# A diffusion block on one core: prologue reordered with two modulation vectors inside it, mixer channels regrouped by shift group, a later w4 load, branch hints on all engines, the last tile in halves

## The chip, the cores and the metric

The kernel runs on one core of a Trainium2 chip. The metric is device time in microseconds (us) of a whole execution; the median of several runs is quoted. Each experiment was timed beside runs of the kernel before on the same chip.

The *span* is the time from the first to the last record of the profiled execution. The time of a run is some 4 to 6 us longer than its span; that difference is called the gap below.

## The reference, cut to what matters

```python
x = A_x                                              # [1, 2048, 640]
mod = (silu(c) @ w_mod).reshape(1, 6, 1, -1)         # six vectors of 640
sa, ca, ga, sb, cb, gb = ...                         # mod[:, 0] ... mod[:, 5]
h = layernorm(x) * (1 + ca) + sa
x = x + ga * attention(h, k_cache, v_cache, wq, wo)  # 32 heads of 128, 2048 keys
h = layernorm(x) * (1 + cb) + sb
u = gelu(layernorm(h) @ w1)                          # 640 channels in 4 groups of 160
u = shift each group by +1, -1, +2, -2 tokens        # group g0 g1 g2 g3
x1 = h + u @ w2
x = x + gb * (x1 + gelu(layernorm(x1) @ w3) @ w4)    # hidden width 1728
```

Two facts of it matter here. Vectors 0 and 1 of the modulation are wanted at once, vectors 2 to 5 only near the end. And a shift group has 160 channels, while a matmul result has 128 partitions, so groups and tiles don't line up.

## The kernel before: the parts that matter

The program is a list of operations with priorities. A small scheduler simulates the engines with assumed durations and fixes, ahead of time, **one order for each engine**; each operation then waits on the chip with semaphores. `slack` is a number of ns that the scheduler adds to the time at which it thinks an operation's inputs are ready; `need` and `from_slot(n)` hold a DMA back until the n-th exponential.

The attention is 128 *steps*: 8 groups of 4 heads, in each group 4 *chunks* of 512 queries, in each chunk 4 heads. A step has 8 pairs of score matmuls, 8 exponentials of 128x1024 on ScalarE, and the PV products.

```python
def ln1(ch, prio):                    # layer norm of chunk ch
    ...
        for i in (a, a + 1):
            ln_stats(xs[i].ap, ..., prio, 0.0 if ch == 0 else 2000.0)     # VectorE
        rstd_act(g, a, a + 2, prio - 100)                                 # ScalarE: Ln, then Exp
        for i in (a, a + 1):
            normed(xn[i].ap, ...)                                         # VectorE
    ...                               # chunk 0: transposes on TensorE; other chunks:
        for i in range(4):
            dmaT(... dma_start_transpose(hT_t[ch][:, :, i * 128:(i + 1) * 128], xn[i].ap), ...)   # SyncE queue
        for k in range(KT):           # VectorE: times (1 + ca), plus sa
            ... hT_t[ch][:, k, :] ...

MS = 17                               # modulation vectors 2, 4, 3, 5 from step 17 on
for n, p in enumerate((2, 4, 3, 5)):
    dma("SP", ... w_half[n % 2] <- w_mod[:, p * D:(p + 1) * D] ...)
    ...                               # 10 matmuls of 128x320 each

def mlp_in(ch, prio):                 # layer norms ahead of the mixer
    tail = ch == NC - 1
    def rstd(g, a):
        if tail:
            rstd_dve(g, a, a + 2, prio)            # last quarter: VectorE, no table
            shift(g, a, a + 2, prio)
        else:
            rstd_act(g, a, a + 2, prio, 1200.0)    # Ln and Exp on ScalarE
            negate(g, a, a + 2, prio, 1200.0)

TAIL = ("A0 WO B0 B1 B2 A1 B3 A2 B4 B5 B6 B7 C0 I3 D0 D1 D2 D3 C1 A3 ...").split()
# A = w1 of a quarter of the rows, B = w2 of a tile, C = w3, D = w4, WO = last attention output product

def w1_part(ch, key):
    for n in range(KT):               # 5 tiles of 128 channels
        ...                           # 5 matmuls of 128x512
        for (p0, p1, dl) in segs[n]:  # a tile is cut where a shift group ends: 9 pieces in all
            P.op("ACT", ... e.activation(us_ap[p0:p1, n, ch * QC + 2 + dl:...], m[p0:p1, :], GELU), ...)
```

Of the kernel before, what the change touches and what calls it, by code (L numbers as in the profile page):

```python
# [40 lines left out]
class Plan:  # L41
# [3 lines left out]
    ENG = ("PE", "ACT", "DVE", "POOL", "SP")  # L45

# [115 lines left out]
    def emit(self, nc, es, ndma, redo, flag):  # L162
# [68 lines left out]
        def body(e):  # L231
            def f(eng):
                for i, o in enumerate(self.seq[e]):
                    if e == "PE" and i == len(self.seq[e]) - 300:
                        hint[e] = eng.mark_branch_hint_location()
                    for sem, v in waits[o].items():
                        eng.wait_ge(sem, v)
                    ins = o.fn(eng)
                    if o.dma:
                        ins.then_inc(o.sem, 16)  # L240
                    elif o.needed:
                        ins.then_inc(o.sem, 1)
                eng.wait_ge(self.flag_op.sem, self.flag_op.semval)
                eng.load(redo[eng.engine], flag[0:1, 0:1])
                for sem in dsem.get(e, ()):
                    if fin.get(sem, 0) > know[e].get(sem, 0):
                        eng.wait_ge(sem, fin[sem])
            return f
# [10 lines left out]
def fast_path(nc, es, flag, A_x, A_k_cache, A_v_cache, A_wq, A_wo, B_w1, B_w2, B_w3, B_w4, c, w_mod, out):  # L259
# [9 lines left out]
    HG = 4  # L269
# [62 lines left out]
    us = [T() for _ in range(NC)]  # L332
# [16 lines left out]
    W12 = [T(), T()]  # L349
    w_half = [W12_t[:, i * KT * D:(i + 1) * KT * D].rearrange("p (k n) -> p k n", k=KT) for i in range(2)]  # L350
# [23 lines left out]
    def dma(eng, fn, kb, reads, writes, prio, need=()):  # L374
        return P.op(eng, fn, {"SP": 480, "ACT": 480, "POOL": 1000}[eng], reads, writes, prio, dma=True, kb=kb, need=need)
# [9 lines left out]
    for i in range(NKV):  # L385
        P.op("POOL", lambda e, i=i: e.memset(V_ap[i][:, :, 128:130], 1.0), 200, (), (V[i],), -297 + i)
# [16 lines left out]
    x0 = load_x2(0, -301) + load_x2(2, -301, eng="ACT")  # L403
# [29 lines left out]
    P.op("DVE", lambda e: e.tensor_copy(s_bc.ap, c_f.ap.unsqueeze(2).to_broadcast([128, KT, 128])), 800, (c_f,), (s_bc,), 0.5)  # L433
    spin(50, -298)
    for k in range(KT):
        def mcol(e, k=k):
            for j in range(2 * KT):
                ins = e.matmul(mc[:, j:j + 1], wm_ap[:, k, j * 128:(j + 1) * 128], s_bf[:, k:k + 1],
                               start=(k == 0 and j == 0), stop=(k == KT - 1), skip_group_check=True)
                if k < KT - 1:  # L440
                    dummy(e, 1)
            return ins
        P.op("PE", mcol, 2 * KT * 120, (wm[k], s_bf, ones), (mc,) + ((warm,) if k < KT - 1 else ()), -290 + k, accum=True)
    spin(12, -281)
# [83 lines left out]
    def ln1(ch, prio):  # L528
        g = ln_slot()
        xs = x0 if ch == 0 else load_x2(4 * ch, XP[ch], from_slot(XS[ch])) + load_x2(4 * ch + 2, XP[ch], from_slot(XS[ch]))  # L530
        for a in (0, 2):
            for i in (a, a + 1):
                ln_stats(xs[i].ap, (xs[i],), g, i, prio, 0.0 if ch == 0 else 2000.0)
            rstd_act(g, a, a + 2, prio - 100)
            for i in (a, a + 1):
                normed(xn[i].ap, xn[i], xs[i].ap, xs[i], g, i, False, prio - 1)
        raw = [T() for _ in range(4)]
        if ch == 0:
# [5 lines left out]
            for i in range(4):  # L544
                def tr(e, i=i):
                    for k in range(KT):
                        ins = e.transpose(hslice(k, i, i + 1), xn[i][:, k * 128:(k + 1) * 128], ident_t[:])
                    return ins
                P.op("PE", tr, 330, (xn[i], ident), (hp[0], hp[1], hq, hp[4]), -280 + i, accum=True)
                spin(6 if i < 3 else 10, -279.5 + i)  # L550
# [18 lines left out]
    def load_k(h, prio, gate=(), need=()):  # L569
        b = h % NKV  # L570
        for i in range(4):
            dmaT(lambda e, i=i: e.dma_start_transpose(K_ap[b][:, i * 512:(i + 1) * 512].unsqueeze(1), A_k_cache[0, h, i * 512:(i + 1) * 512, :]),
                 128, gate, (K[b][i],), prio + 0.01 * i, need)
# [5 lines left out]
    def load_wq(g, a, b, prio, need=()):  # L579
        dma("SP", lambda e: e.dma_start(wq_t[g % 2][:, :, a * 128:b * 128],  # L580
                                        A_wq[:, (g * HG + a) * 128:(g * HG + b) * 128].rearrange("(k p) d -> p k d", p=128)),
            160 * (b - a), (), tuple(wq[g % 2][a:b]), prio, need)
# [8 lines left out]
    load_k(0, -296)  # L591
    load_v(0, -290, "ACT", gate=(wm[3],))
    ln1(0, -280)

    def load_head(h):
# [3 lines left out]
        load_k(h, pr, need=from_slot(n))  # L599
        load_v(h, pr + 1, need=from_slot(n + 1))  # L600
# [6 lines left out]
    load_wq(0, 1, HG, -295)  # L607
# [4 lines left out]


    MS = 17
    for n, p in enumerate((2, 4, 3, 5)):
        dma("SP", lambda e, n=n, p=p: e.dma_start(w_half[n % 2], w_mod[:, p * D:(p + 1) * D].rearrange("(k p) n -> p k n", p=128)),
            800, (), (W12[n % 2],) + (tuple(wm) if n < 2 else ()), MS * NP - 30 + n, from_slot((MS + 2 * n) * NP - 20))
        for hf in range(2):
            m = Tile(pool="M")
            sl = slice(hf * HD, (hf + 1) * HD)  # L620
            for k in range(KT):
                i = (n * 2 + hf) * KT + k
                P.op("PE", lambda e, m=m, sl=sl, k=k, n=n: e.matmul(m[:, 0:HD], s_bc[:, k, :], w_half[n % 2][:, k, sl], start=(k == 0), stop=(k == KT - 1)),  # L623
                     MM(HD), (s_bc, W12[n % 2]), (m,), NP * (MS + i // KT) + 4 + i % KT + 0.65, accum=True)
            P.op("DVE", lambda e, m=m, p=p, hf=hf: e.tensor_scalar_add(out=mod[p][hf].ap, in0=m[:, 0:HD], scalar1=1.0 if p == 4 else 0.0),
                 490, (m,), (mod[p][hf],), NP * MS - 60)

    TAIL = ("A0 WO B0 B1 B2 A1 B3 A2 B4 B5 B6 B7 C0 I3 D0 D1 D2 D3 C1 A3 B8 B9 B10 B11 D4 D5 D6 D7 B12 B13 B14 B15 C2 "
            "D8 D9 D10 D11 C3 D12 D13 D14 D15").split()
    WOKEY = 3000 + 50 * TAIL.index("WO")  # L630
    WOD, CH, I3D = 0, -200, -200


    evac = []
# [13 lines left out]
    def wo_group(g, ch):  # L648
# [3 lines left out]
        for qt in range(4):  # L652
            dmaT(lambda e, qt=qt: e.dma_start_transpose(OT_ap[gs][:, qt], On_ap[gs][:, qt].rearrange("p h d -> p (h d)")),
                 128, (On[gs][qt // 2],), (OT[gs][qt],), s * NP - 100)
# [37 lines left out]
    def step(s):  # L692
# [5 lines left out]
        if s == 0:  # L698
            q_proj(0, [-270 + kk for kk in range(KT)])
            spin(8, -260)  # L700
# [96 lines left out]
    for i, w in enumerate((B_w1, B_w2)):  # L797
        dma("SP", lambda e, i=i, w=w: e.dma_start(w_half[i], w.rearrange("(k p) n -> p k n", p=128)), 800, (), (W12[i],), E)
# [3 lines left out]
    for i, (f0, f1, old) in enumerate(((0, 6, kv(0)), (6, 12, kv(0, 1)))):  # L802
        dma("SP", lambda e, f0=f0, f1=f1: e.dma_start(KV_t[:, f0 * D:f1 * D].rearrange("p (f n) -> p f n", n=D),
                                                      B_w4[f0 * 128:f1 * 128, :].rearrange("(f p) n -> p f n", p=128)),
            960, (), (w4[i],) + old, E + 11 + i)
# [6 lines left out]
    segs = []  # L812
    for n in range(KT):
        lst = []
        p = 0
        while p < 128:
            grp = (n * 128 + p) // G4
            pe_ = min(128, (grp + 1) * G4 - n * 128)
            while p < pe_:
                q1 = min(pe_, p + (128 if p == 0 else (64 if p == 64 else 32)))  # L820
                lst.append((p, q1, DEL[grp]))
                p = q1
        segs.append(lst)
    old = tuple(PT) + tuple(QT)
    P.op("POOL", lambda e: e.memset(us_ap[:, :, 0:4], 0.0), 300, (), (us[0],) + old, -1900)
    P.op("POOL", lambda e: e.memset(us_ap[:, :, UW - 4:UW], 0.0), 300, (), (us[NC - 1],) + old, -1900)

    def w1_part(ch, key):
        for n in range(KT):
            m = Tile(pool="T")  # L830
            for kk in range(KT):
                P.op("PE", lambda e, m=m, n=n, kk=kk: e.matmul(m.ap, w_half[0][:, kk, n * 128:(n + 1) * 128], nT_ap[ch][:, kk, :],  # L832
                                                               start=(kk == 0), stop=(kk == KT - 1)),
                     MM(QC), (W12[0],) + tuple(nT[ch]), (m,), key + n + 0.1 * kk, accum=True)
            for (p0, p1, dl) in segs[n]:
                P.op("ACT", lambda e, m=m, n=n, p0=p0, p1=p1, dl=dl: e.activation(  # L836
                    us_ap[p0:p1, n, ch * QC + 2 + dl:ch * QC + 2 + dl + QC], m[p0:p1, :], GELU), act(QC), (m,), (us[ch],), key)
# [5 lines left out]
    def w2_tile(t, key):  # L843
# [4 lines left out]
        for hf in range(2):  # L848
            for kk in range(KT):
                P.op("PE", lambda e, kk=kk, hf=hf: e.matmul(m[:, hf * 512:hf * 512 + HD], us_ap[:, kk, 2 + t * 128:2 + (t + 1) * 128],  # L850
                                                            w_half[1][:, kk, hf * HD:(hf + 1) * HD], start=(kk == 0), stop=(kk == KT - 1)),
                     MM(HD), tuple(us[x] for x in need) + (W12[1],), (m,), key + hf + 0.1 * kk, accum=True)
# [30 lines left out]
    def w4_tile(t, key):  # L883
        i = t % 4
        b = xb[t]
        m = Tile(pool="W")
        for hf in range(2):
            for f in range(NF):
# [3 lines left out]
                     MM(HD), (gT[f], w4_of(f), w4b), (m,), key + hf + 0.01 * f, accum=True)  # L892
        o_ = xin[t % 4]
# [16 lines left out]
    pr = 2500  # L910
    P.op("DVE", lambda e: e.tensor_reduce(out=fl[:, 0:1], in_=rl_t[:], op=ALU.max, axis=mybir.AxisListType.X), 650, (rl,), (fl,), pr)
    P.op("DVE", lambda e: e.tensor_reduce(out=fl[:, 1:2], in_=rl_t[:], op=ALU.min, axis=mybir.AxisListType.X), 650, (rl,), (fl,), pr)
# [4 lines left out]
    P.op("PE", lambda e: e.matmul(m[:, 0:1], ones.ap, flb.ap, start=True, stop=True), 60, (flb, ones), (m,), 3400)  # L917
# [710 lines left out]
def bass_adaLN_cond__mha_block_cached__mixer_s_mlp__prompt_kernel(  # L1628
    nc, A_x, A_k_cache, A_v_cache, A_wq, A_wo, B_x, B_w1, B_w2, B_w3, B_w4, c, w_mod, out,
):  # L1630
    with nc.sbuf_tensor("flag", [128, 1], I32) as flag:
# [5 lines left out]
        for e, eng in nc.engines.items():  # L1637
            br = eng.br_cmp(redo[e], 0, comp_op="IS_EQ", on_true="done", on_false="general")
            if eng is nc.tensor:
                br.branch_hint(hint["PE"])  # L1640
# [32 lines left out]
```

## Time and profile before

| | before |
|---|---|
| time, median of 3 runs | 1401.2 us |
| profiled run: time, span | 1400.64, 1395.0 us |
| TensorE busy | 1380.7 us |
| first Q projection starts | 14.20 us |
| Q projection of step 4 starts (no wait) | 45.38 us |
| first w1 matmul to last matmul ("the tail") | 1206.27 to 1390.51, 184.2 us |
| last matmul to end of span | 4.5 us |

The page of the profile, parts 1 and 4 (busy time and the chain that ended last), says that TensorE bounds the kernel:

```profile
PE 1380.7 (99%) x13176; PEld 939.8 (67%) x13176; DVE 518.0 (37%) x1337; ACT 1114.6 (80%) x1195; POOL 123.5 (9%) x106
...
PE 96%; ACT 2%; POOL 1%; DVE 0%; DMA 0%; issue 0%; ACTq 0%; POOLq 0%
```

So only what makes TensorE idle, or slow, counts. The view of waits on TensorE of the kernel before (line of code, what it waited for, us in total, times, longest) has little in it:

```profile
PE f_S L668 <- ACT f_PQ L836: 3.2, 1, 3.2
PE f_S L712 <- ACT f_PQ L714: 2.7, 3, 1.8
PE f_S L850 <- ACT f_PQ L836: 1.7, 1, 1.7
```

L836 is the GELU behind w1, in the tail. L712 is a score matmul that waited for an exponential, at 25.5 us.

Now the tail, first as a table of windows (window, its length, busy time and instructions of PE, PEld, DVE, ACT and POOL, granted clock, which is the share of full clock speed that TensorE got, DMA share, GB/s):

```profile
1210.00:1215.00 5.00, 1.83 (x9) 0.62 (x7) 1.08 (x3) 4.89 (x9) 2.51 (x3) 1.00 0.92 193
1215.00:1220.00 5.00, 4.58 (x23) 2.62 (x24) 2.78 (x6) 4.17 (x6) 2.25 (x2) 0.66 0.25 50
...
1230.00:1235.00 5.00, 3.28 (x20) 1.70 (x19) 3.99 (x13) 3.38 (x6) 0.00 (x0) 1.00 0.33 66
```

A window in which TensorE idles over 3 us is followed by one with a granted clock of 0.66; in finer windows that is 0.50 for 3.4 us, from 1215.6 to 1219.0, and 1.00 on both sides. The Trainium skill, "TensorE: Matmul & The Clock Gate", Part 1, says that after an idle window of about 3.4 us the clock is halved, and that the window is free-running; this agrees (3.2 us of waiting, then 3.4 us at 0.50). Half speed over 3.4 us costs at most 1.7 us (an estimate from these two numbers), so **this wait is paid for about one and a half times**. The timeline of the kernel before (start us, duration us, engine, line, operation, out<-in, count, idle time before and its releaser) shows what ScalarE did there:

```profile
1209.28 1.28 ACT L477 ACT_TABLE_LOAD   x1
...
1210.89 1.28 ACT L478 ACT_TABLE_LOAD   x1
...
1212.41 1.28 ACT L836 ACT_TABLE_LOAD   x1
...
1215.04 0.75 PE L668 MATMUL f_S<-f_wo,f_OO 128*128 128x320 bf16 x4 [3.22 <-ACT f_PQ L836]
```

L477 and L478 are Ln and Exp of the third quarter's layer norm. They stand between GELUs, and each of the three changes (to Ln, to Exp, back to GELU) loads a table for 1.28 us.

### The profile page before, as it was taken

The numbers are of one execution on the slowest core, as the hardware profiler recorded it, in microseconds if no ns is written. First come the engines' busy times: TensorE is split into PE (matmuls) and PEld (weight loads), VectorE is DVE, ScalarE is ACT, GpSimd is POOL, SyncE is SP. The second block draws the span as 40 slices with busy tenths as digits, with TensorE's granted clock in tenths as the row PEclk, the third lists the DMA queues.
The fourth block names the chain that finished last, engine by engine and source line by source line (L and its number), as shares of the span: only waits on it lengthen the run. The fifth ranks groups of instructions, "written<-read, shape, count | busy, mean of one in ns | idle before, by whom it ended". The sixth has DMA issues, their size and how long they took to land.

```text
span 1395.0 us, 29964 instructions
## 1 busy us (share of the span) xinstructions
PE 1380.7 (99%) x13176; PEld 939.8 (67%) x13176; DVE 518.0 (37%) x1337; ACT 1114.6 (80%) x1195; POOL 123.5 (9%) x106
## 2 busy tenths in 40 slices
PE   8999999999999999999999999999999999899998
PEld 6666676766676667666776677666766766555554
DVE  4453333233323332333223332333233345595552
ACT  5988888888888888888888888888888888864222
POOL 0000000000000000000000000001233376600000
PEclk9999999999999999999999999999999999999999
DMA  9551623261214221241215112612254112411110
GB/s 203 126 110 34 134 61 85 51 107 35 47 35 88 55 47 35 55 88 33 49 22 98 33 40 33 107 35 47 54 103 102 17 31 55 111 39 48 34 39 24
DMA packets 258963, 88.82 MB, mean 64 GB/s; under 512 B 236625, under 2 KB 257554, under 8 KB 258834
## 3 DMA queue, kind: packets, MB, share of 16 engines
q1 hardware_dynamic: 256210, 85.41, 30.1%
q8 instruction: 104, 1.70, 0.5%
q10 hardware_dynamic: 2624, 1.51, 0.5%
q14 instruction: 25, 0.20, 0.1%
HBM read 43.48 MB, written 2.62 MB: 33 GB/s over the span
## 4 chain that ended last, share of the span: by engine, by line
PE 96%; ACT 2%; POOL 1%; DVE 0%; DMA 0%; issue 0%; ACTq 0%; POOLq 0%
PE f_O L731 33%; PE f_S L712 31%; PE f_M L643 10%; PE f_M L668 10%; PE f_S L890 2%; PE f_M L890 2%; PE f_S L877 2%; PE f_O L877 2%; ACT f_PQ L836 1%; PE f_S L413 1%; PE f_S L850 1%; PE f_M L850 1%; POOL f_y L511 0%; PE f_S L832 0%; PE f_M L623 0%; DMA f_xin<-in_A_x_dram 0%
## 5 line engine op out<-in xcount | busy, mean ns | idle before, releaser
L714 ACT ACTIVATE f_PQ<-f_S 128x1024 bf16<-128x1024 f32 x1024 | 1030.2, 1023 | 155.0 <-PE f_S L712 147.6
L731 PEld LDWEIGHTS f_O<-f_KV,f_PQ 128*128 128x128 bf16 x8192 | 539.6, 98 | 211.4 <-ACT f_PQ L714 0.4
L731 PE MATMUL f_O<-f_KV,f_PQ 128*128 128x129 bf16 x8192 | 612.2, 220 | 0.2 <-ACT f_PQ L714 0.2
L712 PE MATMUL f_S<-f_PQ,f_KV 128*128 128x512 bf16 x2048 | 608.9, 379 | 3.1 <-ACT f_PQ L714 2.7
L676 DVE TENSOR_TENSOR f_y<-f_M,f_y 128x320 f32<-128x320 f32 x192 | 94.4, 492 | 524.8 <-PE f_M L668 524.8
L668 PE MATMUL f_M<-f_wo,f_OO 128*128 128x320 bf16 x992 | 270.2, 299 | 0.0
L712 PEld LDWEIGHTS f_S<-f_PQ,f_KV 128*128 128x128 bf16 x2048 | 192.0, 98 | 46.6 <-ACT f_PQ L714 3.9
L643 PE MATMUL f_M<-f_hT,f_wq 128*128 128x512 bf16 x640 | 159.2, 379 | 0.1
L511 POOL TENSOR_TENSOR f_y<-f_y,f_mod 128x640 f32<-128x640 f32 x40 | 61.3, 1542 | 1058.2 <-DVE f_y L676 1050.8
L668 PEld LDWEIGHTS f_M<-f_wo,f_OO 128*128 128x128 bf16 x992 | 94.9, 97 | 27.9
L643 PEld LDWEIGHTS f_M<-f_hT,f_wq 128*128 128x128 bf16 x640 | 62.4, 98 | 75.9 <-DVE f_hT L557 0.9
L740 DVE TENSOR_TENSOR f_OO<-f_O,f_rl 128x256 bf16<-128x256 f32 x256 | 108.4, 423 | 8.3
L646 DVE CAST f_PQ<-f_M 128x512 bf16<-128x512 f32 x128 | 88.5, 691 | 54.8 <-PE f_M L643 54.7
L738 DVE RECIPROCAL f_rl<-f_O 128x2 f32<-128x2 f32 x256 | 43.5, 170 | 45.9 <-PE f_O L731 41.7
L880 ACT ACTIVATE f_OO<-f_O 128x512 bf16<-128x512 f32 (+1 forms) x28 | 16.7, 596 | 33.2 <-PE f_O L877 33.1
L880 ACT ACTIVATE f_OO<-f_S 128x512 bf16<-128x512 f32 (+1 forms) x28 | 16.6, 595 | 30.7 <-PE f_S L877 30.7
L674 DVE COPY f_y<-f_M 128x320 f32<-128x320 f32 x32 | 15.7, 490 | 67.5 <-PE f_M L668 67.5
L890 PE MATMUL f_S<-f_KV,f_OO 128*128 128x320 bf16 x224 | 34.3, 300 | 0.0
L890 PE MATMUL f_M<-f_KV,f_OO 128*128 128x320 bf16 x224 | 34.3, 300 | 0.0
L472 DVE BATCH_NORM_STATS2 f_small<-f_y 128x6 f32<-128x320 f32 x64 | 29.3, 478 | 10.7 <-POOL f_y L511 10.7
L890 PEld LDWEIGHTS f_M<-f_KV,f_OO 128*128 128x128 bf16 x224 | 20.6, 97 | 14.0 <-issue 5.5
L890 PEld LDWEIGHTS f_S<-f_KV,f_OO 128*128 128x128 bf16 x224 | 20.5, 97 | 13.3 <-issue 4.2
(119 smaller groups left out, 512.5 us busy)
## 6 DMA issues: line engine op xcount, KB each, us to landing
f_KV<-in_A_v_cache_dram SPq DMA_DIRECT2D x31, 512.0 KB, 4.7
f_wo<-in_A_wo_dram SPq DMA_DIRECT2D x8, 640.0 KB, 4.3
f_xin<-in_A_x_dram SPq DMA_DIRECT2D x15, 320.0 KB, 4.1
f_wq<-in_A_wq_dram SPq DMA_DIRECT2D x7, 640.0 KB, 4.6
f_W<-in_w_mod_dram SPq DMA_DIRECT2D x4, 800.0 KB, 4.9
out_dram<-f_xin SPq DMA_DIRECT2D x16, 160.0 KB, 1.8
f_KV<-in_B_w_dram SPq DMA_DIRECT2D x5, 432.0 KB, 3.6
f_KV<-in_A_k_cache_dram SPq DMA_TRANSPOSE x128, 2.8
```

The costliest lines, as they stand in the source:

```text
L511: P.op(eng, lambda e: e.tensor_tensor(out=out, in0=a, in1=b, op=op), COST[eng][0], rd, wr, prio, lat=300 if eng == "POOL" else None)
L643: P.op("PE", lambda e, i=i, kk=kk: e.matmul(m.ap, wq_t[g % 2][:, kk, hh * 128:(hh + 1) * 128], hT_t[ch][:, kk, :], start=(i == 0), stop=(i ...
L646: P.op("DVE", lambda e: e.tensor_copy(q.ap, m.ap), 690, (m,), (q,), s * NP - 90)
L668: P.op("PE", lambda e, m=m, qt=qt, hf=hf, hh=hh: e.matmul(m[:, 0:HD], OT_ap[gs][:, qt, hh, :], wo_t[g % 2][:, hh, hf * HD:(hf + 1) * HD], ...
L676: P.op("DVE", lambda e, m=m, yt=yt: e.tensor_tensor(out=yt.ap, in0=m[:, 0:HD], in1=yt.ap, op=ALU.add), 490, (m, yt), (yt,), s * NP - 60)
L712: P.op("PE", lambda e, sp=sp, r=r, kt=kt: e.matmul(sp[:, r * QC:(r + 1) * QC], K_ap[b][:, kt * 128:(kt + 1) * 128], q.ap, start=True, stop ...
L714: x = P.op("ACT", lambda e, sp=sp, pt=pt: e.activation(pt.ap.rearrange("p k q -> p (k q)"), sp.ap, ACT.Exp, scale=SCALE), 1021, (sp,), (pt ...
L731: ins = e.matmul(o[bk][:, w * 129:w * 129 + 129], pt[:, r, qt * 128:(qt + 1) * 128], V_ap[b][:, u, 0:129], start=(u == 0 and w == 0), stop ...
L738: P.op("DVE", lambda e, ov=ov, i0=i0: e.reciprocal(rl_t[:, i0:i0 + 2].unsqueeze(2), ov[:, 0:258].rearrange("p (u d) -> p u d", u=2)[:, :, ...
L740: evac.append(P.op("DVE", lambda e, ov=ov, i0=i0, bk=bk: e.tensor_tensor(out=On_ap[gs][:, 2 * bk:2 * bk + 2, hh, :], in0=ov[:, 0:258].rear ...
L877: P.op("PE", lambda e, m=m, f=f, kk=kk, fs=fs: e.matmul(m[0:fs, :], w3_ap[:, kk, f * 128:f * 128 + fs], nT_ap[ch][:, kk, :], start=(kk == ...
L890: P.op("PE", lambda e, f=f, hf=hf, fs=fs: e.matmul(m[:, hf * 512:hf * 512 + HD], gT_ap[0:fs, f, i * 128:(i + 1) * 128], w4_ap[f][0:fs, hf ...
```

## The change

Its intent: fill the gaps of the first 20 us with work that has to be done anyway (half of the modulation), start the Q projection earlier, do five full-width GELUs in the mixer instead of nine pieces, shorten the end, and have each engine's last branch hinted ahead. The core of the diff:

```diff
 # prologue
-        P.op("DVE", ... s_bc <- c_f broadcast, 800, ...)
+        P.op("POOL", ... s_bc <- c_f broadcast, 1000, ...)
-    spin(12, -281)                       # and three other groups of warm-up matmuls
-            rstd_act(g, a, a + 2, prio - 100)
+            rstd_act(g, a, a + 2, prio - 100, 0.0 if ch == 0 else 1500.0)      # slack
-    load_v(0, -290, "ACT", gate=(wm[3],))
+    for p, b, pools, keys in ((2, NKV - 1, ("O0", "O1"), (-262, 0.5)), (4, NKV - 2, ("M", "M"), (1.5, 2.2))):
+        dma("ACT", ... K/V buffer b <- mod_src(p), 800 KB, gate wm[1] ...)      # vectors 2 and 4, early
+        for hf in range(2): modulation(p, hf, ...)
+        if p == 4: load_v(0, -290, "ACT", gate=(wm[1],))                        # V of head 0 behind them
-    MS = 17                              # four vectors from step 17 on
-    for n, p in enumerate((2, 4, 3, 5)): ...
+    for n, p in enumerate((3, 5)):       # two vectors, loaded at exponential 8 and 20, used in steps 2 to 5
+        dma("SP", ... w_half[n] <- mod_src(p) ..., 8 + 12 * n, from_slot(8 + 12 * n))
 # mixer
-    TAIL = ("A0 WO B0 B1 B2 A1 B3 A2 B4 B5 B6 B7 C0 I3 D0 ...
+    TAIL = ("A0 B0 B1 B2 A1 B3 WO B4 B5 A2 B6 I3 B7 B8 C0 B9 D0 ...
-        for n in range(KT):              # 9 GELU pieces
+        for n in (4, 0, 1, 2, 3):        # tile 4 = the last 32 channels of each group; 0..3 = the first 128
+            if n == 4: one GELU into `rest`, then 4 VectorE copies of 32 partitions, shifted
+            else:      one GELU of 128x512, shifted
-            960, (), (w4[i],) + old, E + 11 + i)
+            960, (), (w4[i],) + old, E + 11 + i, after=last_ot if i else ())    # later w4 load
 # end
+            if last: two VectorE passes and an output DMA for each half of 320 columns
 # all engines
-            if eng is nc.tensor: br.branch_hint(hint["PE"])
+            (every engine) .branch_hint(hint[name])
```

## The prediction

> **What bounds it now.** TensorE: busy 1380.7 of 1395.0 us (the profile's first part), and the chain that ended last is 96% PE. Start-to-start spacings from the timeline (0.216 us for 512 columns, 0.136 for 320, 0.057 for 129, 0.151 for w4) times their counts give an estimated 1360 us of matmuls that the change doesn't remove. About 35 us of the span is left to win, plus 6.2 us between span (1395.0) and time (1401.2); over 2% (28 us) is nearly impossible.
>
> **Where the 35 us lie** (timeline, table of windows):
> - Prologue: the first Q projection starts at 14.2 us, after warm-up matmuls that fill waits (the last 40 cost about 2 us between 10.7 and 13.6). Then PE waits 0.3, 0.7 and 1.8 us, the last because VectorE stood 4.5 us waiting for x with the Q copy queued behind.
> - Modulation: 40 matmuls, 5.4 us, from step 17 on, where PE is full.
> - Start of the tail: PE idle 3.2, 0.4 and 1.7 us (1211.8 to 1232.7), by ScalarE: 9 GELU pieces of 0.59 us per quarter of the rows, table loads of 1.28 us, a first GELU that waits 1.2 us for a memset. After the 3.2 us gap the granted clock reads 0.66 in a 5 us window, about 1.5 us more. The Trainium skill ("TensorE: Matmul & The Clock Gate", Part 1) says an idle window of about 3.4 us halves the clock; the trace agrees.
> - End: two VectorE passes of 0.82 us and an output transfer (1.8 us) after the last matmul.
>
> **What the change does.**
> - Prologue: drops 48 warm-up matmuls, takes a broadcast (0.80 us) off VectorE, transposes two tiles before the last column product. Q projection near 12.5 (-1.7).
> - Half of the modulation (20 matmuls, 2.7 us) moves into gaps while the first exponentials run; about 2 us becomes free. The VectorE stall goes: the Q copy stands before the statistics (-1.8). Against this, 1.6 MB of w_mod stand ahead of the first V load on the ScalarE queue; V took 7.1 us to land; I expect it near 20 us, about when the first PV product (20.2 before) wants it. Net -5.
> - Mixer: 5 GELUs a quarter instead of 9, the first without the memset; the attention output product moves behind four w2 tiles, the late w4 load (7.5 us) behind the last transposes; four VectorE copies of 0.33 us are added. Two pairs of Ln/Exp table loads stay between the GELUs, so 2 to 3 us of PE wait remain. Net -3.
> - Last tile in halves: 0.49 + 0.49 instead of 0.82 + 0.82 us: -0.7.
> - Hints: only SP's branch comes last, after the final landing. The skill ("Runtime: NRT & Kernel Launch", Instruction fetch mechanics) says a taken branch outside the fetched pages must fetch its target; no profile here shows its cost. I allow -1, outside the span.
>
> Sum -9.7: **1391.5 us**, 80% range **1386 to 1397**. Chances: faster 0.01, same 0.98, slower 0.01.
>
> **What would show it.** First Q projection near 12.5; no PE wait over 1 us from 20 to 30; 20 modulation matmuls before 20 us; 20 w1 GELUs instead of 36; PE idle from 1200 to 1240 below 3.5 us, no window there below 0.8 clock; span 8.7 shorter, its gap to the time 1 shorter.
>
> **What would make it wrong.** w_mod or V landing late, with PE standing before the first scores (gain near zero); Ln/Exp table loads standing before the second quarter's GELUs longer than I allow; VectorE, with added copies, becoming the releaser in the tail; a hint worth nothing or several us.

## More of the kernel before

A fixed order means that an operation behind a late one is late too, even if its own inputs are there.

Steps 0 to 3 are chunk 0, step 4 is the first of chunk 1.

A step's Q projection is done during the step ahead of it, so the Q projection of step 4 is the first matmul that needs chunk 1's normalised and transposed x (`hT`).

How chunk 1 came to TensorE can be followed in the timeline of the kernel before (start us, duration us, engine, line, operation, out<-in, count, idle time before and its releaser):

```profile
20.90 1.77 DVE L472 BATCH_NORM_STATS2 f_small<-f_xin 128x6 f32<-128x320 bf16 x4 [4.46 <-DMA f_xin<-in_A_x_dram]
...
24.34 0.20 ACT L477 ACTIVATE f_small<-f_small 128x2 f32<-128x2 f32 x1 [2.03 <-DVE f_small L473]
...
26.73 6.10 SPq L562 DMA_TRANSPOSE f_hT<-f_xn  x4
...
34.20 1.71 DVE L564 TENSOR_SCALAR f_hT<-f_hT,f_small 128x512 bf16<-128x512 bf16 x5 [3.19 <-DMA f_hT<-f_xn]
...
45.38 1.24 PE L643 MATMUL f_M<-f_hT,f_wq 128*128 128x512 bf16 x5
```

VectorE stood 4.46 us for x (the stall that the change wants to remove). But the rest of the chain ran early: Ln at 24.3, transposes issued from 26.7, `hT` finished at 35.9, and TensorE wanted it at 45.4. There were 9.5 us in hand.

## The result and the profile after

| | before | after |
|---|---|---|
| time, median (runs) | 1401.14 us (4) | 1408.01 us (4) |
| profiled run: time, span, gap | 1400.64, 1395.0, 5.6 | 1407.93, 1403.4, 4.5 |
| first Q projection | 14.20 | 13.39 |
| Q projection of step 4 | 45.38 | 50.03 |
| tail | 184.2 us | 187.8 us |
| last matmul to end of span | 4.5 us | 4.2 us |

The ratio of after to before is 1.0049, with a 95% interval of 1.0031 to 1.0066. The change costs about 7 us where a gain of 9.7 was predicted.

Where it went can be read from the starts of the Q projections, one per step, after minus before:

| step | 0 | 1 | 3 | 4 | 5 | 7 | 18 | 26 and later |
|---|---|---|---|---|---|---|---|---|
| us | -0.8 | +0.4 | +0.4 | +4.65 | +8.7 | +10.5 | +10.5 | +5.1 |

From step 18 to 26 the new kernel gains 5.4 us, because its modulation matmuls were done before. Of the 10.5 us, four half vectors within steps 3 to 6 account for 2.7 us. The net loss ahead of the tail is 5.1 us. The tail adds 3.6 us (its first w1 record is missing from the trace of after; its start is taken as 1206.27 + 5.08 us, which is one matmul of 0.216 us ahead of the first record that is there). With -0.3 us at the end, the sum is the 8.4 us of span; the gap gives back 1.1.

In the page of after, TensorE has 12901 matmul records instead of 13176, because some are missing from the trace; so its busy sums are not compared.

The view of waits on TensorE of the kernel after names the places:

```profile
PE f_M L655 <- DVE f_hT L566: 3.9, 2, 3.4
PE f_S L864 <- ACT f_PQ L851: 3.3, 1, 3.3
PE f_M L864 <- ACT f_PQ L851: 2.7, 3, 2.4
PE f_O L742 <- DMA f_KV<-in_A_v_cache_dram: 2.0, 1, 2.0
PE f_M L655 <- DVE f_hT L559: 1.1, 1, 1.1
```

The wait on exponentials at 25.5 us is gone, as intended. In its place there is a wait of 3.9 us for `hT` (chunk 1, at step 4), and one of 2.0 us for V of head 0; and in the tail two waits of 2.7 and 3.3 us where before had 3.2, 0.4 and 1.7. The timeline of after shows how chunk 1 came late, the same chain as shown of before:

```profile
22.17 0.89 DVE L475 BATCH_NORM_STATS2 f_small<-f_xin 128x6 f32<-128x320 bf16 x2 [1.15 <-DMA f_xin<-in_A_x_dram]
...
28.93 0.17 DVE L749 RECIPROCAL f_rl<-f_O 128x2 f32<-128x2 f32 x1 [4.43 <-PE f_O L742]
29.02 0.19 DVE L476 BATCH_NORM_AGGREGATE f_small<-f_small 128x2 f32<-128x12 f32 x1
...
32.93 0.20 ACT L480 ACTIVATE f_small<-f_small 128x2 f32<-128x2 f32 x1
...
39.50 2.60 SPq L564 DMA_TRANSPOSE f_hT<-f_xn  x2
...
42.76 4.36 SPq L564 DMA_TRANSPOSE f_hT<-f_xn  x2
...
49.56 0.41 DVE L566 TENSOR_SCALAR f_hT<-f_hT,f_small 128x512 bf16<-128x512 bf16 x1 [4.88 <-DMA f_hT<-f_xn]
50.03 0.61 PE L655 MATMUL f_M<-f_hT,f_wq 128*128 128x512 bf16 x1 [3.44 <-DVE f_hT L566]
```

The first statistics start only 1.3 us later than before (22.17 instead of 20.90). Then VectorE stands 4.43 us at a reciprocal that waits for TensorE, with the aggregation of the first two tiles (29.0 and 30.0 us; before at 24.0) and the last three statistics behind it. ScalarE runs the Ln at 32.9 instead of 24.3; its inputs were there at 30.2, and ScalarE has no idle time before it, which means that it stood in its fixed order behind exponentials. The transposes are issued at 39.5 instead of 26.7, and `hT` comes 3.4 us too late. The windows of after show the second payment, at 50 us and in the tail:

```profile
45.00:50.00 5.00, 1.53 (x16) 0.85 (x14) 0.44 (x3) 2.58 (x3) 0.00 (x0) 0.94 1.13 152
50.00:55.00 5.00, 4.53 (x17) 1.91 (x18) 3.87 (x13) 0.96 (x1) 0.00 (x0) 0.50 0.61 215
...
1215.00:1220.00 5.00, 2.47 (x12) 0.98 (x10) 1.88 (x6) 4.93 (x9) 2.52 (x4) 1.00 0.55 103
1220.00:1225.00 5.00, 4.82 (x24) 2.86 (x24) 1.89 (x3) 0.32 (x1) 2.30 (x2) 0.66 0.68 208
...
1230.00:1235.00 5.00, 1.70 (x9) 0.60 (x7) 1.82 (x11) 4.93 (x8) 1.74 (x2) 0.88 0.00 1
1235.00:1240.00 5.00, 4.96 (x20) 2.71 (x20) 2.71 (x7) 1.07 (x2) 0.00 (x0) 0.50 0.17 34
```

The granted clock is 0.50 over 50 to 55 us and again over 1235 to 1240, and 0.66 over 1220 to 1225. In finer windows these are stretches of 6.8 us (from 49.4 and 1233.8) and of 3.4 us (from 1220.1), each at 0.50: TensorE is busy there, at half speed. And the timeline of the tail of after, first quarter:

```profile
1214.33 1.28 ACT L480 ACT_TABLE_LOAD   x1
...
1215.93 1.28 ACT L481 ACT_TABLE_LOAD   x1
...
1217.45 1.28 ACT L851 ACT_TABLE_LOAD   x1
...
1219.40 0.31 PE L864 MATMUL f_M<-f_W,f_PQ 128*128 128x320 bf16 x1 [2.35 <-ACT f_PQ L851]
```

There are 20 GELUs instead of 36, as planned, but the Ln and Exp, with their three table loads, come in the middle of a quarter's five GELUs, with the w2 product waiting for the last three. The second quarter repeats it (loads from 1229.65 on, wait of 3.3 us ending at 1234.72).

### The profile page after: what moved, and what is told of

Same layout as the page of the kernel before. It is cut to its first block, busy times and chain, and to the rows that moved or that the text cites. A ratio compares the mean times of both kernels' runs of the same rounds, so it can differ in the third digit from the quotient of the medians.

```text
span 1403.4 us, 29645 instructions
## 1 busy us (share of the span) xinstructions
PE 1371.6 (98%) x12901; PEld 939.5 (67%) x13128; DVE 524.9 (37%) x1354; ACT 1106.3 (79%) x1179; POOL 125.3 (9%) x108
## 4 chain that ended last, share of the span: by engine, by line
PE 95%; DMA 2%; ACT 1%; issue 1%; DVE 0%; ACTq 0%; SPq 0%
PE f_O L742 33%; PE f_S L723 30%; PE f_M L680 10%; PE f_M L655 10%; PE f_M L905 3%; PE f_S L891 2%; PE f_O L891 2%; PE f_S L905 2%; DMA f_KV<-in_A_v_cache_dram 1%; PE f_S L864 1%; PE f_M L864 1%; DMA f_W<-in_w_mod_dram 1%; PE f_S L841 1%; PE f_O L841 1%; ACT f_PQ L725 0%
## 5 line engine op out<-in xcount | busy, mean ns | idle before, releaser
L723 PE MATMUL f_S<-f_PQ,f_KV 128*128 128x512 bf16 x1873 | 572.2, 379 | 9.4 <-ACT f_PQ L725 0.2
L894 ACT ACTIVATE f_OO<-f_O 128x512 bf16<-128x512 f32 x28 | 16.7, 596 | 35.9 <-PE f_O L891 35.9
L905 PE MATMUL f_M<-f_KV,f_OO 128*128 128x320 bf16 x252 | 38.6, 300 | 0.0
L520 ACT ACTIVATE f_xn<-f_y,f_small 128x640 bf16<-128x640 f32 x12 | 10.7, 915 | 26.1 <-DVE f_small L499 21.8
L905 PE MATMUL f_S<-f_KV,f_OO 128*128 128x320 bf16 x196 | 30.0, 300 | 0.0
```

Of the source, the lines that this page charges most:

```text
L723: P.op("PE", lambda e, sp=sp, r=r, kt=kt: e.matmul(sp[:, r * QC:(r + 1) * QC], K_ap[b][:, kt * 128:(kt + 1) * 128], q.ap, start=True, stop ...
L905: P.op("PE", lambda e, f=f, hf=hf, fs=fs: e.matmul(m[:, hf * 512:hf * 512 + HD], gT_ap[0:fs, f, i * 128:(i + 1) * 128], w4_ap[f][0:fs, hf ...
```

## The experiments

The theory after reading the two traces: two orders are at fault, one in the prologue (chunk 1's layer norm pushed back in ScalarE's and SyncE's order, by the slack and by the loads ahead of it) and one in the tail (table exchanges in the middle of a quarter), and each wait of over about 3 us is doubled by the clock. Rivals: that the early modulation traffic on the DMA engines is the cause in the prologue, wherever the orders put it; that the regrouping itself is worth nothing; that the hints cost time.

### The parts alone: p_only, m_only, h_only, l_only

Each is the kernel before with one group of the diff's hunks: the prologue; the mixer with its order and later w4 load; the hints; the last tile in halves. (In m_only, part of w2 lands where modulation vectors were, so those loads were made to wait for the modulation matmuls; a first build without that had a race.)

> Before plus the prologue part alone. The traces of before and after put the start of the Q projection of step 27 at +5.1 us, so theory A (the parts add, and the prologue is the larger loss) expects about 1406 us, with the first PE wait over 3 us at step 4's Q projection again. Rival B (the prologue is a gain by itself, as predicted at -5, and is only spoilt by the mixer's early weight loads at 60 us) expects about 1396 us.

> Before plus the mixer's regrouping, the new order of the tail and the later w4 load alone. From the first w1 matmul to the last matmul it was 184.2 us before and 187.8 after; theory A expects the same +3.6, about 1404.7 us, with two PE waits of 2 to 3 us behind GELUs that stand behind Ln and Exp table loads. Rival B (the tail lost only because it arrived after a slower clock or at another moment of the GpSimd chain) expects the predicted -3, about 1398 us.

> Before plus the branch hints alone. The gap between span and time went from 5.6 us (profiled run of before) to 4.2 to 5.3 (runs of after), so theory A expects about -1 us, 1400.1, with the span unchanged at 1395.0. Rival B: the gap only scatters from run to run, and the time is unchanged within 0.3 us.

> Before plus the last tile in halves alone. Prediction: -0.7 us in the span. The trace of after shows from the end of the last matmul to the end of the span 4.2 us against 4.5 before, so theory A expects only -0.3, since two output transfers and their issue (0.33 us each) take back part; within noise of 1401.

| run | time, median | before, same rounds | ratio (95%) | what the trace shows |
|---|---|---|---|---|
| p_only | 1405.3 | 1400.69 | 1.0032 (1.0015 to 1.0048) | wait for `hT` 4.0 us, for V 1.9 us |
| m_only | 1403.38 | 1400.69 | 1.0016 (0.9999 to 1.0033) | waits 3.3 and 2.7 us, tail 187.9 us |
| h_only | 1400.26 | 1400.69 | 0.9994 (0.9977 to 1.0011) | gaps 5.6, 4.4, 4.6, 4.8 us; before 5.2 to 6.2 |
| l_only | 1399.4 | 1400.69 | 0.9990 (0.9973 to 1.0006) | last matmul to end 3.7 us (before 4.5) |

The parts add: +4.6, +2.7, -0.4 and -1.3 us make +5.6, against +6.9 for the whole, within the spread of the runs. The view of waits of p_only shows the same two waits in the prologue as after:

```profile
PE f_M L654 <- DVE f_hT L565: 4.0, 2, 3.6
...
PE f_O L741 <- DMA f_KV<-in_A_v_cache_dram: 1.9, 1, 1.9
```

So the prologue and the mixer are at fault separately. The halves give about 1 us, 0.9 of it behind the last matmul; all four spans of l_only lie in 1393.7 to 1393.9, and before's lowest of these rounds was 1394.6. The hints shorten the gap by about 1 us in three of four runs, but the time of that run alone doesn't resolve it. Over all runs the median gap is 4.8 us with the hints (45 runs, 4.1 to 5.8) and 5.6 without (47 runs, 5.0 to 6.2).

### a_warm: keep the waits, take away the slow clock

```diff
+        if s == 4: 58 matmuls of ones, ahead of the Q projection          # result overwritten
+        ... 40 and 56 of them in the two w2 products that wait in the tail
```

> After, with warm-up matmuls of 128 columns placed in its three long PE waits (58 ahead of step 4's Q projection, 40 and 56 inside the first and fourth w2 tile); no semaphore wait is taken away. Theory clock: each wait costs about double its length, because the granted clock drops for some 3.4 us behind it (trace of after: 0.69 in 50 to 60, 0.66 in 1220 to 1225, 0.50 in 1235 to 1240); kept busy, PE stays at 1.00 there and the kernel gains about 3 + 1.5 + 3, so near 1401. Rival: the slow stretches come from something else (data arriving late, DMA load), and the time stays at 1408 within 1 us.

Measured: 1403.9 us, ratio 1.0021 (1.0004 to 1.0038), so about 3.9 us better than after. The windows show a clock of 1.00 everywhere that after had 0.50 to 0.66; steps 4 to 5 took 9.2 us instead of 12.3, and the tail 185.0 instead of 187.8. For instance, the window that had 0.50 in after:

```profile
50.00:55.00 5.00, 4.80 (x60) 3.49 (x58) 3.70 (x12) 0.93 (x2) 0.00 (x0) 1.00 0.75 247
```

The slow clock is real: steps 4 to 5 and the tail together became 5.9 us shorter. The run as a whole gained only 3.9, and not the 7 expected, because in the profiled run the wait for V at the start was longer (2.4 us) and was itself followed by 3.4 us at 0.50, from 24.2 us on, which the dummies didn't cover; a new wait for VectorE (0.6 us) came up too. The dummy matmuls don't shorten a wait; they only keep its price single.

### a_slack0: undo one number

```diff
-            rstd_act(g, a, a + 2, prio - 100, 0.0 if ch == 0 else 1500.0)
+            rstd_act(g, a, a + 2, prio - 100)
```

> After, with only the added 1500 ns of slack on the statistics of the later row chunks undone; the plan then puts the first Ln two exponentials earlier on ScalarE and two pairs of hT transposes between the K loads of head 3 on SP. Theory order: step 4's Q projection waited because of where ScalarE and SP had those instructions in their fixed order; the 3.4 us wait and the slow clock behind it go, about -6, near 1402. Theory load: it waited because the queue carries more bytes than before by then; the wait stays above 2 us and the time within 2 us of 1408.

Measured: 1403.15 us, ratio 1.0019 (1.0002 to 1.0036), about 4.2 us better than after. The view of waits:

```profile
PE f_O L742 <- DMA f_KV<-in_A_v_cache_dram: 4.1, 2, 2.2
```

The wait for `hT` and its slow clock are gone. The 95% intervals of this run and of after overlap, but no single time does (1401.8 to 1404.0 against 1406.9 to 1409.0), and in the trace the Q projection of step 26 starts 4.8 us earlier than in after. A second wait for V (up to 2.2 us) takes part of the gain: chunk 1's transposes now go ahead of a V load on the same queue. The order theory holds for the wait, but with no margin: VectorE begins to scale `hT` at 45.02 us, against 49.56 in after and 34.20 in before, and TensorE takes it at 46.51. The slack accounts for the last 4.5 of 15.4 us of lateness. It moves ScalarE's and SyncE's orders together, so the two are not told apart.

The trace also shows how much the price of a wait can vary. The first w2 product waits here as long as in after, and yet the clock stays up:

```profile
1214.56 0.31 PE L864 MATMUL f_M<-f_W,f_PQ 128*128 128x320 bf16 x1 [2.36 <-ACT f_PQ L851]
```

```profile
1215.00:1220.00 5.00, 4.77 (x32) 3.14 (x33) 3.13 (x5) 0.48 (x1) 2.47 (x2) 1.00 0.69 195
```

The stretch from the last Q projection to the last matmul is 1.4 us shorter than in after for that reason. In m_only the clock fell behind this same wait, in a_wm3late and a_vfirst it did not. That fits a window that runs freely; it is also luck, and not a part of the repair.

### a_wm3late: take one load away from that stretch

```diff
-        dma("SP", ... w_half[n] ..., 8 + 12 * n, from_slot(8 + 12 * n))
+        dma("SP", ... w_half[n] ..., 60 + 12 * n, from_slot(60 + 12 * n))
         # and their matmuls 8 steps later
```

> After, with the loads of modulation vectors 3 and 5 and their 20 matmuls put some 50 exponentials later (the load of vector 3 left the SP queue at 31.7 us, in front of head 3's K and the hT transposes). Theory load: 0.8 MB less ahead of the hT transposes shortens the wait at step 4 from 3.4 us to about 1 and leaves the clock up, about -5 us, near 1403. Theory order: the transposes also waited for x to be normalized (39.1 us), which this doesn't move, so the wait shrinks by less than 1.5 us.

Measured: 1407.68 us (1404.37 to 1411.7), ratio 1.0059 (1.0039 to 1.0079). The wait for `hT` was still 4.0 us (longest 3.6), and the Q projection of step 4 started at 49.48 us instead of 50.03. So the load of vector 3 is not what makes chunk 1 late. Whether the edit gains time isn't shown: the times of this run scatter more than others, which I can't explain, and the profiled one is the fastest of the four.

### a_dve2: no table exchange in the mixer

```diff
+            elif ch == NC - 2:
+                rstd_dve(g, a, a + 2, prio)        # the same function that the last quarter uses
+                negate(g, a, a + 2, prio, 1200.0)
```

> After, with the two inverse standard deviations of the third row chunk's mixer input computed on VectorE (as the last chunk's already are) instead of by Ln and Exp on ScalarE, so no table is exchanged between the GELUs of the tail. Theory tables: both PE waits in the tail (2.4 and 3.3 us) and the slow clock behind them go, about -9 us, near 1399, with 2 table loads after 1205 us at most. Rival: the waits have VectorE or GpSimd behind the tables as the next releaser and shrink by less than half, 1404 or more.

Measured: 1402.84 us, ratio 1.0012 (0.9996 to 1.0029), about 5.2 us better than after. The tail took 181.3 us (after 187.8, before 184.2), with a granted clock of 1.00 in every window. Two of its windows, to be compared with those of 0.66 and 0.50 in after:

```profile
1220.00:1225.00 5.00, 3.31 (x23) 1.85 (x21) 4.72 (x16) 0.69 (x2) 2.57 (x3) 1.00 0.74 223
...
1235.00:1240.00 5.00, 3.51 (x25) 1.91 (x23) 5.00 (x17) 0.92 (x1) 0.00 (x0) 1.00 0.43 84
```

The waits that remain in the tail are 0.3 to 0.8 us each, most of them on VectorE, which is 94% and 100% busy in these windows: it has become the next limit there. (Part of the tail's 6.5 us was lost again in the prologue of that run, where the wait for `hT` was 5.2 us: its step 26 starts 3.2 us later than in after, with the same prologue. So a difference of 3 us between single traces can be noise.)

### a_vfirst: head 0's V ahead of one modulation vector

```diff
-    load_v(0, -290, "ACT", gate=(wm[1],))
+    load_v(0, -291.5, "ACT", gate=(wm[1],))       # between vectors 2 and 4; vector 4's matmuls later
```

> After, with the first V load put ahead of modulation vector 4's weights on the ScalarE queue, and vector 4's 10 matmuls moved from before the third scores to behind the first PV products. Theory V: the 2.0 us that the first PV product waited for V at 22.7 us were the price of the 0.8 MB ahead of it; the wait goes, 1.4 us of matmuls leave the gap, so -0.5 to -2 us in the first 30 us, time near 1406.5 while the wait at step 4 stays. Rival: the DMA engines are shared whatever the order, V lands within 1 us of the old time and the wait stays.

Measured: 1407.85 us, ratio 1.0041 (1.0023 to 1.0059): no gain. The wait for V is gone, but the timeline of this run shows something that neither theory had:

```profile
7.10 5.51 ACTq L610 DMA_DIRECT2D f_KV<-in_w_mod_dram  x1
12.66 0.20 ACT L480 ACTIVATE f_small<-f_small 128x2 f32<-128x2 f32 x1 [7.85 <-issue]
```

The last of the three large loads on ScalarE's queue took 5.51 us to issue, and ScalarE could not run chunk 0's Ln (at 8.02 us in after) until 12.66. TensorE then waited 3.6 us for chunk 0, and the first Q projection began at 17.55, at a clock of 0.50 from 15.1 on for 6.8 us. What held up the issue isn't in the trace. Here an issue held its engine; three large loads ahead of the first layer norm on the engine that the layer norm needs is a gamble on the DMA engines' load.

### a_sd and a_sdv: both repairs, and V first

a_sd has the edits of a_slack0 and a_dve2; a_sdv has a_vfirst's as well.

> After with both repairs that each gained alone: the slack undone (-4.2 us by the ratios) and the third chunk's standard deviations on VectorE (-5.2). If the two stages are independent, -9.4 from 1407.7: about 1398.3, already below before. If the gain of one fills a wait of the other, above 1400.

> The same two repairs and V first. Theory V adds 0.5 to 2 us to them: about 1397. Rival (shared DMA engines): equal to the run without V first within 0.5 us.

Measured: a_sd 1398.64 us, ratio 0.9984 (0.9967 to 1.0001); a_sdv 1398.81 us, ratio 0.9984 (0.9968 to 1.0001). The two repairs add: from after's +6.9 to -2.3 us. So undoing the slack and the exchanges more than makes up for the loss. That doesn't make them its only causes: in a_sd TensorE still waits 1.6 us for `hT` at step 4, with 3.4 us at 0.50 behind it, because the repaired order leaves no margin: `hT` is scaled from 48.41 us on. (In a_dve2, which differs by the slack alone, it was 53.05, so the slack is worth some 4.6 us of lateness here too.) V first again neither gains nor loses; in a_sdv the wait for chunk 0 is 4.7 us, and yet the time is a_sd's.

### x_late: is doing the modulation early worth anything?

a_sd, but all four modulation vectors back at step 17 and later, as before; the first V load keeps its earlier gate.

> The rest of the change kept with both repairs, but all four modulation vectors loaded and computed where before had them (step 17 on), so 2.4 MB of w_mod leave the first 50 us and 20 matmuls (2.7 us) go back where PE is full. If the early w_mod traffic costs more than the 2.7 us that the gaps can hide: about 1394, under the run with the two repairs alone by 2 us or more. If the gaps are worth their traffic: 1 to 3 us above it.

Measured: 1395.95 us, ratio 0.9962 (0.9946 to 0.9979), 2.7 us better than a_sd in the same rounds (the intervals overlap; the starts of step 26 in the traces differ by 2.7 us too). The central idea of the change, filling gaps with early modulation, costs more than it hides in these two plans: 2.4 MB of weights are added in the first 50 us, ahead of or among the loads of the first heads, where the DMA share of the kernel before is already 1.2 to 1.4 (windows from 10 to 25 us; the view adds up the times of packets, so it can exceed 1). VectorE begins to scale chunk 1's `hT` at 38.11 us here and at 48.41 in a_sd, so early modulation, with the orders that it brings, is behind the larger part of that chunk's lateness. Load and order change together here and aren't told apart. A new wait appeared. The timeline of x_late, SyncE's queue and TensorE:

```profile
36.75 3.96 SPq L574 DMA_TRANSPOSE f_KV<-in_A_k_cache_dram  x3
40.76 0.58 SPq L579 DMA_DIRECT2D f_KV<-in_A_v_cache_dram  x1
...
45.81 1.03 PE L739 MATMUL f_O<-f_KV,f_PQ 128*128 128x129 bf16 x8 [2.41 <-DMA f_KV<-in_A_v_cache_dram]
```

Head 3's V is issued at 40.76, behind K and chunk 1's transposes, and lands too late; the wait is followed by 3.4 us at 0.50. This left two questions open: whether that is order or load, and what the regrouped mixer gives by itself, since the kernel before has table exchanges in its tail too.

### b_dve2: the table exchanges taken from the old mixer

The kernel before with a_dve2's edit alone.

> The kernel before, with one edit: the Ln and Exp of the third quarter's layer norm are replaced by VectorE operations, so that no activation table is exchanged between the first quarters' GELUs. Theory A (the table exchanges were the whole difference, and the regrouping of mixer channels by itself gives nothing): the stage from the first w1 matmul to the last matmul takes 181 to 182.5 us, and the time is about 1398.5 (before minus 2 to 3 us). Theory B (the regrouping is worth what was predicted, some 2 to 3 us, once the exchanges are gone): the stage stays at 183 to 184.5 us and the time at 1400 to 1401.5, because the nine GELU pieces of a quarter hold ScalarE. The prologue is not touched: all Q projections before step 127 as in the kernel before, to 0.3 us.

Measured: 1400.27 us, ratio 0.9995 (0.9981 to 1.0008); tail 1206.19 to 1390.14 us, 183.95 us. The view of waits:

```profile
PE f_S L853 <- ACT f_PQ L839: 2.4, 2, 1.7
PE f_S L668 <- DMA f_OO<-f_OO: 1.8, 1, 1.8
```

In the old order, the same edit is worth 0.3 us of tail, in the new one 6.5. The 3.2 us wait of before is gone, but a wait for the transposed attention output, which it had hidden, takes its place (1.8 us), and with shorter ones the sum is about what it was. So Theory B: without exchanges, the regrouped mixer takes 181.3 us against 183.95, and is worth about 2.6 us. Its order of tiles and the later w4 load come with it in every run, so the three aren't told apart.

### x_v3: one issue moved

x_late, with head 3's V issued behind the first two transposes of chunk 1.

> x_late with one edit: on the SyncE queue, head 3's V load is issued after the first two transposes of chunk 1 instead of after head 3's last K transpose, so some 8 us earlier (near 33 instead of 40.8). Theory A (the wait of 2.4 us for V at 45.8 is the place in the queue): the wait goes, the fifth Q projection keeps its start to about 1 us, and the time is 1393 to 1394.5 (x_late minus 1.5 to 2.4). Theory B (the DMA engines are full in that stretch and the wait only moves): V waits or waits for chunk 1's transposes of about the same sum, 1.5 to 2.5 us, and the time 1395.5 to 1396.5.

Measured: 1394.41 us, ratio 0.9957 (0.9943 to 0.9970). The timeline shows the issue, and no wait on V is left in the view of waits (the longest left, apart from the start's 1.0, is 0.9 us):

```profile
33.51 0.53 SPq L579 DMA_DIRECT2D f_KV<-in_A_v_cache_dram  x1
```

The Q projection of step 4 starts later, at 43.23 us instead of 41.73, and a wait of 0.9 us for K came up; but that of step 5 starts at 51.41 us instead of 53.97 (before: 53.56), and the median span falls from 1391.3 to 1389.4 us. So it was mostly order and not load: the wait of 2.4 us and the slow clock behind it went, and 1.5 us came back ahead of it, 0.5 of them before the first Q projection. Between x_late and x_v3, on two chips, the intervals of the ratios overlap, so the traces show the gain better than the times do. This kernel beats both: 6.5 us under the kernel before in the same rounds, and 13.6 under the median of the kernel after, which was taken in other rounds.

## Why the prediction was wrong

**Prologue: predicted -5, measured +5.1.** The step that failed is "The VectorE stall goes: the Q copy stands before the statistics (-1.8) ... Net -5". The 4.46 us stall for x shrank to 1.15, and the 1.8 us wait on exponentials went. But the statistics and everything behind them (Ln, normalisation, transposes) moved later in fixed orders, and I followed them only as far as 30 us. The 9.5 us that before had in hand at step 4 were gone, plus 3.4. The comparison of the two orders, which I had, showed the Ln behind more exponentials and the transposes behind K of head 3; I read what the change did to the first consumer (step 0 and 1), not to the next user of the same engines. a_slack0 shows that the order makes the wait: with one number undone it is gone. But the slack explains only the last 4.5 us of the lateness; x_late shows that most of the rest goes with the early modulation. So the step "about 2 us becomes free" failed too: with the modulation back at step 17 the repaired kernel is 2.7 us faster.

**V late: named, placed some 2.5 us too early, and left out of the sum.** I wrote that V would land "near 20 us, about when the first PV product (20.2 before) wants it". It landed at 22.7, a wait of 2.0 us. V's issue to landing was about 16 us with two vectors of 800 KB ahead of it on ScalarE's queue, against 7.1 before. That waiting in the DMA queues fits the Trainium skill, "DMA: Bandwidth & Descriptors", Queues, rings and completion order, which says that each DMA engine takes turns between the queues it has work for: K's transposes on SyncE's queue take their share of the same time. The traces show the size of each: V took 8.3 us with no vector ahead of it on its queue (x_late), 12.1 with one (a_vfirst) and 15.9 with two (after), so each vector ahead of it cost about 4 us.

**Mixer: predicted -3, measured +3.6.** The step that failed is "Two pairs of Ln/Exp table loads stay between the GELUs, so 2 to 3 us of PE wait remain. Net -3". The waits measured 2.7 and 3.3 us, 6.0 in all, and behind them the clock was 0.50 for 3.4 and 6.8 us. The predicted -3 is about what the mixer gives when there are no exchanges at all (181.3 us against 184.2). I took the gain of fewer GELUs in full and then allowed for the exchanges as if they were independent of the order. They were not: the same edit that removes them is worth 0.3 us in the old order and 6.5 in the new. In the new one, the product that waits needs the GELUs behind the exchange at once.

**The clock.** I priced one slow window in before (1.5 us) as something to gain, and none in after. a_warm's trace is 5.9 us shorter in the two places where after had three slow stretches, and its time 3.9 us shorter.

**What held.** 20 GELUs instead of 36; 20 modulation matmuls before 20 us; an earlier Q projection (13.39, -0.8 us instead of -1.7, as TensorE waited 1.1 us for the scaled x). The last tile in halves was predicted at -0.7 and measured alone at about -1.2 in the span, of which -0.9 behind the last matmul (in after itself, -0.3). The hints, allowed at -1 outside the span, show a gap 0.8 us shorter in the median of all runs. The Trainium skill, "Runtime: NRT & Kernel Launch", Instruction fetch mechanics, says that a taken branch whose target is not in the current pages forces a fetch before execution goes on; the shorter gap agrees, but the gap's content is not in a trace.

**What stays open.** Why a_wm3late's times scatter over 7 us; whether early modulation costs by its bytes or by the orders that come with it; which of regrouping, order of tiles and w4 load makes the new mixer wait behind the exchanges. The end of the span is 3.7 us in l_only and 4.2 in after, although the last output lands 2.7 us after the last matmul in both (3.5 in before). The records between differ in SyncE's branch, which is hinted in after only: the drain behind it begins 0.46 us after the branch in after and 0.12 in l_only (h_only 0.27, before 0.13). So the hints seem to cost a little inside the span; one trace of each doesn't prove it.

## What to carry to other kernels

With fixed orders, moving an operation moves everything behind it on that engine: follow each displaced chain to its consumer, also the one 20 us later, and ask how much time it had in hand. Price a wait of 3 us or more at one and a half to two times its length where TensorE is the bound, expect that a shorter one may cost extra too, and look for the clock in the window *after* it. And a cost that two orders share (here two exchanges of three table loads each) may be free in one and dear in the other, so it has to be read from what waits behind it, not from its duration.

## What the Trainium skill lacked or had wrong

- "ScalarE: Activation LUTs", What ACT_TABLE_LOAD costs: it gives 1283 ns for the load, which agrees with the 1.28 us here, plus a drain of about 1380 ns, 2.66 us for each switch. No such drain shows in these traces: in the kernel after, loads start at 1214.33, 1215.93 and 1217.45, 1.5 to 1.6 us apart with a small Ln or Exp between them, so a switch with its small operation took 1.6 us in all.
- "DMA: Bandwidth & Descriptors": I found no figure for how long an issue may hold its engine when the DMA engines are loaded. Here an issue on ScalarE's queue took about 0.5 us each for two loads and 5.51 us for the third (a_vfirst), with ScalarE's own work standing behind it; four DMA transposes of K took 5.7 to 6.8 us to issue between 16 and 40 us in the kernel after, where a single one in x_v3, at 50.7 us, took 1.12.
- "TensorE: Matmul & The Clock Gate", Part 1: its figure of about 3.4 us is borne out as a length: up to the last matmul every slow stretch in these traces lasts 3.4 or 6.8 us, at 0.50. It is no lower limit for a wait, though: every wait of 3.2 us or more was followed by such a stretch, the wait of 2.4 us in the tail was in after and m_only and was not in a_slack0, a_wm3late and a_vfirst, and in a_sd two idle pieces of 1.4 and 0.3 us were enough.
